# Attention products in three bursts per two rounds, row maxima in parts of 512, 512 and 1024 keys

## The chip, the core and the metric

The kernel runs on one core of one Trainium2 chip. The metric is the device time of one execution in microseconds (us). The core has TensorE (PE in the profile, with its weight loads shown apart as PEld), VectorE (DVE), ScalarE (ACT), GpSimd (POOL) and SyncE (SP, which here issues nearly all DMAs). TensorE writes its results to PSUM, which has eight banks; one bank holds 512 fp32 values on each of 128 partitions.

## The reference

Two attention blocks (A and B) of 32 heads with 16 dimensions each work on the same 2048 x 512 input, each with its own weights, and a gate per row mixes their results. Cut to what matters:

```python
def _A_ref(x, wqkv, wo):                      # _B_ref is the same with B's weights
    qkv = (x @ wqkv).reshape(B, S, 3, H, Dh)  # S = 2048, H = 32, Dh = 16
    scores = einsum("bhqd,bhkd->bhqk", q, k) * Dh ** -0.5
    p = softmax(scores, axis=-1)
    o = einsum("bhqk,bhkd->bhqd", p, v)
    return o.transpose(...).reshape(B, S, D) @ wo

g = sigmoid((x * gate_w).sum(-1, keepdims=True))
out = g * a + (1 - g) * b                     # a, b: the two blocks on A_x
```

## The kernel before

**Stages.** A prologue (up to about 294 us of the trace) makes q, k and v of both blocks (`project_qk`, `project_v`) and writes them to DRAM, q and k as a high and a low part, so that one matmul with 48 rows gives a precise product. Then 1024 rounds follow, 64 heads (both blocks) of 16 rounds each; a round r is one tile of 128 keys against all 2048 queries of a head. A tail of some 50 us finishes the output.

**One round.** It has three kinds of work:

1. *Scores and exponentials* (`scores`, L549 and L552). Four matmuls of 512 queries give the scores of 128 keys, with keys on partitions. The row maximum of each query enters as two more rows of the same matmul (50 rows in all). ACT takes each 512-wide result from its bank with one `Exp` into the tile `p`. The banks are `ps_st`, three of them in turn.
2. *Products with V* (`attend`, L521), one round behind: `acc` (one bank) collects p times V for the head. The 17 columns of V (16 and a column of ones for the sum) need few columns of the array, so four matmuls with `tile_position=(0, 32*c)` stand beside each other, one for each quarter of the queries. A *burst* is such a group: before the change it covers 256 columns of each quarter, and there are two bursts a round. The operands are plain fp32, and the trace shows each such matmul as two MATMUL records (8 records a burst).
3. *Row maxima* for a later head (`max_half`, L112 and L114), 20 rounds ahead (NT + LEAD = 16 + 4): a tile of 128 queries against all 2048 keys, as two halves of 1024 keys. A half is two matmuls of 512 into the two banks of one `ps_mx` tile (two such tiles) and one DVE `tensor_reduce` over 1024. After 16 tiles `max_split` (L124) joins the halves on DVE, POOL splits the result in two parts, and `max_rows` (L131) transposes them and sends them through DRAM into the two extra rows of `q_st`.

**Places in the array.** The stacked q and k lie twice, on partitions 0 to 49 and 64 to 113 (`HALVES`), so that two matmuls with 48 or 50 rows stand in the upper and the lower half of the array at once. Scores and maxima therefore come in pairs, and TensorE goes back and forth between this arrangement and that of the bursts.

**What sets the order.** Nothing is scheduled by a planner: each engine takes its instructions in the order in which the program issues them (`manual_schedule`), and waits come from buffers. The body of a round before is

```python
for half in range(2):
    pair(r, (2 * half, 2 * half + 1))
    if m < ROUNDS:
        max_half(m, half)
    if r:
        attend(r - 1, half)
```

A half-round is thus: a pair of scores, a pair of maxima, a burst. Work that comes now and then is in the table `later` (by round): loads of V and of output weights, denominators (`load_den`, `invert_den`), normalising, the output projection (`project_out`, 32 times within the rounds), the gate. At a head's last round ACT copies `acc` to `ev` (L538); the first burst of the next head waits for it, as there is one `acc`. While the last 20 rounds run there are no more maxima to make.

PSUM before: two `ps_mx` tiles (four banks), three `ps_st`, one `acc`. All eight are taken.

## Time and profile before

| | before |
|---|---|
| median of 3 runs | 2935.14 us (2934.06 to 2935.32) |
| the profiled execution: time, its span | 2934.63 us, 2932.8 us |
| granted TensorE clock | 0.999 |
| PE, DVE, ACT busy (share of the span) | 99%, 89%, 79% |
| DMA | 73 GB/s mean |

Busy shares are of records in the trace. Records of one engine overlap: a MATMUL's record goes from the fetch of its operands to the end of its writes, and the next one begins long before. A PE that is busy 99% of the time is therefore not a PE without gaps, and for DVE and ACT too the distance from one start to the next says more than the length of a record. The lines of the profile follow in the prediction.

### The profile page before, as it was taken

What the parts mean: (1) busy time and instruction counts of PE and PEld (TensorE: products, weight loads), DVE (VectorE), ACT (ScalarE), POOL (GpSimd) and SP (SyncE); (2) the same over time, 40 slices, a digit from 0 to 9 for tenths busy, and PEclk for the clock granted to TensorE, in tenths of its full rate; (3) what the DMA queues carried; (4) which work ended last, traced back from release to release, by engine and by line L of the source; (5) the groups of instructions that cost most, each with busy time, mean ns of one, the idle gap of its engine ahead of it and who ended that gap; (6) DMA issues with size and microseconds to landing.
All of it is one profiled execution on the core that took longest, in us unless ns stands there. A gap on an engine that the chain in (4) does not pass through costs nothing.

```text
span 2932.8 us, 61642 instructions
## 1 busy us (share of the span) xinstructions
PE 2905.4 (99%) x26192; PEld 1199.9 (41%) x26192; DVE 2618.4 (89%) x2343; ACT 2321.2 (79%) x4257; POOL 224.4 (8%) x369
## 2 busy tenths in 40 slices
PE   8999999999999999999999999999999999999999
PEld 7877333333333333333333444333333333334435
DVE  3145999999999999999999988999999999998884
ACT  3221888888888888888888776888888888887775
POOL 1000231000000000000100231000000000011201
PEclk9999999999999999999999999999999999999999
DMA  7662333222322232222323241222222233232302
GB/s 246 190 229 115 78 78 79 53 46 38 66 53 54 54 64 50 39 50 52 82 53 63 76 113 39 53 55 53 58 39 53 52 72 64 53 71 77 74 6 89
DMA packets 83753, 214.61 MB, mean 73 GB/s; under 512 B 21878, under 2 KB 32086, under 8 KB 70934
## 3 DMA queue, kind: packets, MB, share of 16 engines
q1 hardware_dynamic: 80918, 201.76, 30.1%
q0 software_dynamic: 2560, 8.91, 1.2%
q8 instruction: 206, 3.38, 0.5%
q14 instruction: 69, 0.57, 0.1%
HBM read 145.87 MB, written 64.74 MB: 72 GB/s over the span
## 4 chain that ended last, share of the span: by engine, by line
PE 95%; ACT 3%; issue 1%; DMA 1%; DVE 0%; SPq 0%
PE acc L521 38%; PE ps_st L549 29%; PE ps_mx L112 16%; PE ps_pro L195 6%; PE ps_mx L404 3%; PE ps_pro L218 3%; ACT p L552 1%; ACT ev L538 1%; DMA raw<-in_xT 0%; DMA k_st<-kd 0%; PE ps_st L404 0%; PE ps_st L455 0%; PE ps_mx L455 0%; DVE mxp L114 0%; DVE o_acc L456 0%
## 5 line engine op out<-in xcount | busy, mean ns | idle before, releaser
L114 DVE TENSOR_REDUCE mxp<-ps_mx 128x1 f32<-128x1024 f32 x2048 | 2485.9, 1222 | 41.6 <-PE ps_mx L112 40.4
L552 ACT ACTIVATE p<-ps_st 128x512 f32<-128x512 f32 x4096 | 2224.3, 596 | 360.1 <-PE ps_st L549 115.0
L521 PE MATMUL acc<-p,vg 128*17 128x256 f32 x16384 | 1285.1, 385 | 14.1 <-ACT ev L538 12.7
L549 PE MATMUL ps_st<-q_st,k_st 50*128 50x512 f32 x4096 | 1027.0, 496 | 0.0
L112 PE MATMUL ps_mx<-k_st,q_st 48*128 48x512 f32 x4096 | 821.0, 395 | 1.7 <-DVE mxp L114 1.4
L549 PEld LDWEIGHTS ps_st<-q_st,k_st 50*128 50x128 f32 x4096 | 385.3, 183 | 866.2 <-issue 453.0
L521 PEld LDWEIGHTS acc<-p,vg 128*17 128x17 f32 x16384 | 272.7, 95 | 754.8 <-issue 711.4
L112 PEld LDWEIGHTS ps_mx<-k_st,q_st 48*128 48x128 f32 x4096 | 397.6, 187 | 15.5 <-issue 9.0
L125 POOL CAST mparts<-mrow 128x16 fp32r<-128x16 f32 x64 | 12.5, 196 | 2261.8 <-DVE mrow L124 2261.8
L200 DVE TENSOR_TENSOR part<-ps_pro,part 128x1024 fp32r<-128x1024 f32 x32 | 39.2, 1224 | 109.6 <-ACT part L199 109.6
L199 ACT CAST part<-ps_pro 128x1024 fp32r<-128x1024 f32 x32 | 32.4, 1014 | 131.4 <-PE ps_pro L195 131.4
L404 PE MATMUL ps_mx<-wo,ot 128*128 128x512 f32 (+1 forms) x354 | 91.1, 402 | 0.0
L195 PE MATMUL ps_pro<-xh,whi 128*128 128x512 f32 x256 | 73.1, 405 | 7.9 <-ACT xh L181 7.5
L221 ACT COPY v_st<-ps_pro 128x512 f32<-128x512 f32 x31 | 18.2, 587 | 77.5 <-PE ps_pro L218 75.1
L404 PEld LDWEIGHTS ps_mx<-wo,ot 128*128 128x128 f32 (+1 forms) x354 | 64.0, 188 | 26.1 <-DVE mxp L114 10.2
L195 PE MATMUL ps_pro<-xh,wlo 128*128 128x512 f32 x256 | 69.4, 393 | 0.0
L195 PE MATMUL ps_pro<-xl,whi 128*128 128x512 f32 x256 | 69.3, 393 | 0.0
L195 PEld LDWEIGHTS ps_pro<-xh,whi 128*128 128x128 f32 x256 | 47.9, 191 | 22.5 <-ACT xh L181 9.9
L195 PEld LDWEIGHTS ps_pro<-xh,wlo 128*128 128x128 f32 x256 | 48.7, 190 | 10.4
L195 PEld LDWEIGHTS ps_pro<-xl,whi 128*128 128x128 f32 x256 | 48.6, 190 | 10.3
L169 DVE TENSOR_TENSOR wlo<-wraw,whi 128x512 fp32r<-128x512 f32 x16 | 10.9, 683 | 46.8 <-ACT whi L168 46.8
L408 DVE TENSOR_SCALAR o_acc<-ps_mx,gate 128x512 f32<-128x512 f32 x16 | 12.0, 751 | 35.8 <-PE ps_mx L404 35.8
(89 smaller groups left out, 603.5 us busy)
## 6 DMA issues: line engine op xcount, KB each, us to landing
k_st<-kd SPq DMA_DIRECT2D x128, 256.0 KB
q_st<-qd SPq DMA_DIRECT2D x128, 256.0 KB
qd<-part SPq DMA_DIRECT2D x32, 512.0 KB
kd<-part SPq DMA_DIRECT2D x32, 512.0 KB
k_st<-kd SPq DMA_DIRECT2D x128, 128.0 KB
q_st<-qd SPq DMA_DIRECT2D x128, 128.0 KB
od<-ev SPq DMA_DIRECT2D x63, 256.0 KB
vd<-v_st SPq DMA_DIRECT2D x32, 272.0 KB
```

What stands on the lines that cost most here:

```text
L112: pe.matmul(ps[:, c * 512:(c + 1) * 512], q[b:b + SC, t * P:(t + 1) * P], k[b:b + SC, o:o + 512], start=True, stop=True)
L114: dve.tensor_reduce(mxp[h][:, t, half:half + 1], ps, op=ALU.max, axis=AX.X)
L195: pe.matmul(ps[:, c * 512:(c + 1) * 512], a[:, k], b[:, k], start=n == 0, stop=n == 3 * KC - 1)
L199: act.copy(pt[0], ps)
L200: dve.tensor_tensor(pt[1], ps, pt[0].bitcast(F32), op=ALU.subtract)
L218: pe.matmul(ps[:, :DM], a[:, k, o:o + P], b[:, k], start=n == 0, stop=n == 3 * KC - 1)
L221: act.copy(v_st[t % 2][:, :, 0:16], v)
L404: pe.matmul(ps, ot[a][:n, slot, sl], wt[b][:n, g], start=G == groups[0] and i == 0, stop=G == groups[-1] and i == 2)
L521: pe.matmul(acc[32 * c:32 * c + 17, half * 256:(half + 1) * 256], v[:, 4 * a + c if final else kt, j], p[:, o:o + 256], start=first and ha ...
L538: act.copy(ev, acc)
L549: pe.matmul(ps[:, i * 512:(i + 1) * 512], k[b:b + SC + 2, kk * P:(kk + 1) * P], q[b:b + SC + 2, cc * 512:(cc + 1) * 512], start=True, stop ...
L552: act.activation(pt[r][:, o:o + n], ps[:, :n], AF.Exp, scale=SCALE)
```

## The change

Two rounds form one step of the loop, and a string gives the order of what PE is handed: `e` is one score matmul with its exponential, `m` a part of the maxima of 512 keys, `M` one of 1024 keys, and a digit is a burst of so many units of 128 columns. The two rounds' products come in three bursts of 384, 256 and 384 columns, and lie up to two rounds behind the scores. The maxima of one tile come as parts of 512, 512 and 1024 keys; the 512 parts use two tiles `ps_m1` of one bank, the 1024 part a single tile `ps_m2` of two banks (together the four banks that `ps_mx` had). The half of the array (`rows`) now alternates from matmul to matmul after each burst. `max_split` joins three partial maxima in place of two. In the last 20 rounds the string is `LATE`. The prologue's early maxima (`run_ahead`) are handed out in parts, `load_den` and `invert_den` move by one or two rounds, and `project_out` stands ahead of a step's first burst.

On PE, in the steady part of the rounds, these rows stood before (names: `ps_st` is a bank of scores, `ps_mx` a tile for maxima, `acc` the bank of the products, `17x256 x4` a burst):

```order
L549 MATMUL ps_st<-q_st_1967,k_st_1968 128x512 x2
L112 MATMUL ps_mx<-k_st_111,q_st_110 128x512 x2
L521 MATMUL acc<-p,vg 17x256 x4
L549 MATMUL ps_st<-q_st_1967,k_st_1968 128x512 x2
L112 MATMUL ps_mx<-k_st_111,q_st_110 128x512 x2
L521 MATMUL acc<-p,vg 17x256 x4
```

That is one round; two rounds have four bursts, each behind two pairs. Now, from a step's first burst to its third (`ps_m_` with a number is a tile of `ps_m1` or, where two matmuls write it, of `ps_m2`):

```order
L532 MATMUL acc<-p,vg 17x384 x4
L571 MATMUL ps_st<-q_st_2010,k_st_2011 128x512 x2
L123 MATMUL ps_m_18783<-k_st_114,q_st_113 128x512
L123 MATMUL ps_m_18786<-k_st_114,q_st_113 128x512
L532 MATMUL acc<-p,vg 17x128 x8
L571 MATMUL ps_st<-q_st_2010,k_st_2011 128x512
L123 MATMUL ps_m_18800<-k_st_114,q_st_113 128x512 x2
L571 MATMUL ps_st<-q_st_2010,k_st_2011 128x512
L123 MATMUL ps_m_18808<-k_st_114,q_st_113 128x512
L571 MATMUL ps_st<-q_st_2010,k_st_2011 128x512
L532 MATMUL acc<-p,vg 17x384 x4
```

Three bursts stand in two rounds, with two, three and three pairs between them. The middle burst is eight matmuls of 128 columns, since it takes the last 128 of one round and the first 128 of the next.

On DVE, in the same part, one row before was one half of 1024 keys:

```order
L114 TENSOR_REDUCE mxp_3380<-ps_mx_3517 128x1
L114 TENSOR_REDUCE mxp_3380<-ps_mx_3531 128x1
L114 TENSOR_REDUCE mxp_3380<-ps_mx_3549 128x1
L114 TENSOR_REDUCE mxp_3380<-ps_mx_3563 128x1
```

and those of two rounds are now six, four of 512 (`ps_m1`) and two of 1024 (`ps_m2`):

```order
L125 TENSOR_REDUCE mxp_10843<-ps_m2_11187 128x1
L125 TENSOR_REDUCE mxp_10843<-ps_m1_11195 128x1
L125 TENSOR_REDUCE mxp_10843<-ps_m1_11208 128x1
L125 TENSOR_REDUCE mxp_10843<-ps_m2_11214 128x1
L125 TENSOR_REDUCE mxp_10843<-ps_m1_11232 128x1
L125 TENSOR_REDUCE mxp_10843<-ps_m1_11235 128x1
```

The same columns are read, in six instructions where there were four, and the two large ones have one tile between them.

The diff:

```diff
--- before.py
+++ after.py
@@ -58,7 +58,8 @@
     const = ctx.enter_context(tc.tile_pool(name="const", bufs=1))
     small = ctx.enter_context(tc.tile_pool(name="small", bufs=2))
     dram = ctx.enter_context(tc.tile_pool(name="dram", bufs=1, space=DRAM))
-    ps_mx = ctx.enter_context(tc.tile_pool(name="ps_mx", bufs=2, space=PSUM))
+    ps_m1 = ctx.enter_context(tc.tile_pool(name="ps_m1", bufs=2, space=PSUM))
+    ps_m2 = ctx.enter_context(tc.tile_pool(name="ps_m2", bufs=1, space=PSUM))
     qd = [[dram.tile([2, HG, DH, S], F32, name=f"qd{s}{g}") for g in range(NG)] for s in range(2)]
     kd = [[dram.tile([2, HG, DH, S], F32, name=f"kd{s}{g}") for g in range(NG)] for s in range(2)]
@@ -99,19 +100,29 @@
             dma(k[b + 32:b + 48].bitcast(F32), ks[0, j])
             dma(q[b + 32:b + 48].bitcast(F32), qs[1, j])
+    PARTS = ((0,), (1,), (2, 3))
     mxp = {}
-    def max_half(m, half):
+    turn = [0]
+    def rows():
+        turn[0] ^= 1
+        return HALVES[1 - turn[0]]
+    def max_part(m, part):
         h, t = divmod(m, NT)
-        if t == 0 and half == 0:
-            mxp[h] = small.tile([P, NT, 2], F32, name="mxp")
+        if t == 0 and part == 0:
+            mxp[h] = small.tile([P, NT, 3], F32, name="mxp")
         q, k = q_st[h % 3], k_st[h % 3]
-        ps = ps_mx.tile([P, 1024], F32, name="ps_mx")
-        for c in range(2):
-            o, b = half * 1024 + c * 512, HALVES[c]
-            pe.matmul(ps[:, c * 512:(c + 1) * 512], q[b:b + SC, t * P:(t + 1) * P], k[b:b + SC, o:o + 512],
-                      start=True, stop=True)
-        dve.tensor_reduce(mxp[h][:, t, half:half + 1], ps, op=ALU.max, axis=AX.X)
+        chunks = PARTS[part]
+        n = len(chunks)
+        ps = (ps_m1 if n == 1 else ps_m2).tile([P, n * 512], F32, name=f"ps_m{n}")
+        for i, c in enumerate(chunks):
+            b = rows()
+            pe.matmul(ps[:, i * 512:(i + 1) * 512], q[b:b + SC, t * P:(t + 1) * P],
+                      k[b:b + SC, c * 512:(c + 1) * 512], start=True, stop=True)
+        dve.tensor_reduce(mxp[h][:, t, part:part + 1], ps, op=ALU.max, axis=AX.X)
@@ -121,7 +132,7 @@
         halves = mxp.pop(h)
         m = small.tile([P, NT], F32, name="mrow")
         mp = small.tile([P, 2, NT], F32R, name="mparts")
-        dve.tensor_tensor(m, halves[:, :, 0], halves[:, :, 1], op=ALU.max)
+        dve.tensor_reduce(m, halves, op=ALU.max, axis=AX.X)
         pool.tensor_copy(mp[:, 0], m)
         pool.tensor_tensor(mp[:, 1], m, mp[:, 0].bitcast(F32), op=ALU.subtract)
         mparts[h] = mp
@@ -211,7 +222,7 @@
             hi, lo = wblocks[s, 2 * DM]
             c, o = divmod(t * P, 512)
             last = s == 1 and t == NT - 1
-            ps = ps_mx.tile([P, 1024], F32, name="ps_mx") if last else ps_pro.tile([P, 1024], F32, name="ps_pro")
+            ps = ps_m1.tile([P, 512], F32, name="ps_m1") if last else ps_pro.tile([P, 1024], F32, name="ps_pro")
             n = 0
             for a, b in ((xh[c], hi), (xl[c], hi), (xh[c], lo)):
                 for k in range(KC):
@@ -236,13 +247,14 @@
             split_x(c, 2, load_x(c, 2))
             if c < 3:
                 block(load_w, c)
-        ahead = [(m, half) for m in range(NT + LEAD) for half in range(2)]
+        ahead = [(m, part) for m in range(NT + LEAD) for part in range(3)]
         def run_ahead(n):
-            for _ in range(min(n, len(ahead))):
-                m, half = ahead.pop(0)
-                max_half(m, half)
-                if (m, half) == (NT - 1, 1):
+            turn[0] = 0
+            for _ in range(n):
+                m, part = ahead.pop(0)
+                max_part(m, part)
+                if (m, part) == (NT - 1, 2):
                     max_split(0)
                     pending.append(0)
@@ -254,7 +266,7 @@
                 load_w(i // 8, 2 * DM, DM)
             if i in (4, 9):
                 split_w(i // 8, 2 * DM, DM)
-            project_qk(s, g, isk, lambda: run_ahead(i >= 10))
+            project_qk(s, g, isk, lambda: run_ahead((i >= 10) + (i >= 13)))
             if i in (5, 6, 8, 9):
                 load_stacks(i // 8, HALVES[(i - 5) % 3:][:1])
             if i == 7:
@@ -270,7 +282,7 @@
                 if pending[0] == 3:
                     max_rows(pending.pop() - 3)
             if t and t != NT - 2:
-                run_ahead(2)
+                run_ahead(3)
         assert not ahead and not pending
@@ -389,7 +401,7 @@
     def result_bank():
         banks.append(len(banks) % 5)
         if banks[-1] % 2 or not fill_only:
-            return ps_mx.tile([P, 1024], F32, name="ps_mx")[:, :DM]
+            return ps_m1.tile([P, 512], F32, name="ps_m1")
         return ps_st.tile([P, 512], F32, name="ps_st")
     def project_out(side, t):
@@ -475,7 +487,7 @@
         end = (G + 1) * HG * NT
         at(end + 2, load_den, G)
         at(end + 10, invert_den, G, 0)
-        at(end + 11, invert_den, G, 1)
+        at(end + 12, invert_den, G, 1)
     for side in range(2):
         groups = SIDES[side]
         end = (groups[-1] + 1) * HG * NT
@@ -489,9 +501,9 @@
             for i in range(4):
                 at(end + 42 + 16 * c + 2 * i, project_out, side, 4 * c + i)
     end = ROUNDS - NT
-    at(end + 1, load_den, LAST)
+    at(end + 2, load_den, LAST)
     for i in range(2):
-        at(end + 3, invert_den, LAST, i)
+        at(end + 4, invert_den, LAST, i)
     fill = []
     for c in range(NQ):
         at(end + 4 + c // 2, load_num, LAST, c)
@@ -509,7 +521,7 @@
-    def attend(r, half):
+    def attend(r, qa, qb):
         h, kt = divmod(r, NT)
         v, j = vg[h // HG], h % HG
         p = pt[r]
@@ -517,11 +529,10 @@
         a = kt % 4
         first, last = (a == 0, a == 3) if final else (kt == 0, kt == NT - 1)
         for c in range(NQ):
-            o = c * 512 + half * 256
-            pe.matmul(acc[32 * c:32 * c + 17, half * 256:(half + 1) * 256],
-                      v[:, 4 * a + c if final else kt, j], p[:, o:o + 256],
-                      start=first and half == 0, stop=last, tile_position=(0, 32 * c), skip_group_check=True)
-        if half == 0:
+            pe.matmul(acc[32 * c:32 * c + 17, qa * P:qb * P], v[:, 4 * a + c if final else kt, j],
+                      p[:, c * 512 + qa * P:c * 512 + qb * P], start=first and qa == 0, stop=last,
+                      tile_position=(0, 32 * c), skip_group_check=True)
+        if qb < 4:
             return
         del pt[r]
         if final and last:
@@ -538,49 +549,69 @@
             act.copy(ev, acc)
             nc.sync.dma_start(od[G][j].rearrange("c r t -> (c r) t"), ev)
+    done = [0]
+    def attend_next(n):
+        while n:
+            r, qa = divmod(done[0], 4)
+            qb = min(4, qa + n)
+            attend(r, qa, qb)
+            done[0] += qb - qa
+            n -= qb - qa
+    def score(r, c):
+        h, kt = divmod(r, NT)
+        if c == 0:
+            pt[r] = ppool.tile([P, S], F32, name="p")
+        q, k = q_st[h % 3], k_st[h % 3]
+        kk, cc = (4 * (kt % 4) + c, kt // 4) if h == NH - 1 else (kt, c)
+        b = rows()
+        ps = ps_st.tile([P, 512], F32, name="ps_st")
+        pe.matmul(ps, k[b:b + SC + 2, kk * P:(kk + 1) * P], q[b:b + SC + 2, cc * 512:(cc + 1) * 512],
+                  start=True, stop=True)
+        act.activation(pt[r][:, c * 512:(c + 1) * 512], ps, AF.Exp, scale=SCALE)
+    FULL = "e3eemm2eMeme3emeM"
+    LATE = "ee2ee2ee2ee2"
     after = {}
-    def scores(r, chunks, ps):
+    for r in range(0, ROUNDS, 2):
         h, kt = divmod(r, NT)
-        q, k = q_st[h % 3], k_st[h % 3]
-        for i, c in enumerate(chunks):
-            kk, cc = (4 * (kt % 4) + c, kt // 4) if h == NH - 1 else (kt, c)
-            b = HALVES[c % 2]
-            pe.matmul(ps[:, i * 512:(i + 1) * 512], k[b:b + SC + 2, kk * P:(kk + 1) * P],
-                      q[b:b + SC + 2, cc * 512:(cc + 1) * 512], start=True, stop=True)
-        o, n = chunks[0] * 512, len(chunks) * 512
-        act.activation(pt[r][:, o:o + n], ps[:, :n], AF.Exp, scale=SCALE)
-    def one():
-        return ps_st.tile([P, 512], F32, name="ps_st")
-    def pair(r, chunks):
-        for c in chunks:
-            scores(r, (c,), one())
-    for r in range(ROUNDS + 1):
-        for fn, a in later.pop(r, ()):
-            fn(*a)
-        h, kt = divmod(r, NT)
+        projects = []
+        for rr in (r, r + 1):
+            for fn, a in later.pop(rr, ()):
+                if fn is project_out:
+                    projects.append(a)
+                else:
+                    fn(*a)
+        if kt == 0 and h + 2 < NH:
+            load_stacks(h + 2)
         m = r + NT + LEAD
-        if r < ROUNDS:
-            if kt == 0 and h + 2 < NH:
-                load_stacks(h + 2)
-            pt[r] = ppool.tile([P, S], F32, name="p")
-            for half in range(2):
-                pair(r, (2 * half, 2 * half + 1))
-                if m < ROUNDS:
-                    max_half(m, half)
+        scored = parts = 0
+        for step in FULL if m < ROUNDS else LATE:
+            if step == "e":
+                score(r + scored // 4, scored % 4)
+                scored += 1
+            elif step in "mM":
+                max_part(m + parts // 3, parts % 3)
+                parts += 1
+            else:
+                for a in projects:
+                    project_out(*a)
+                projects = []
+                turn[0] = 0
                 if r:
-                    attend(r - 1, half)
-            if m < ROUNDS and m % NT == NT - 1:
-                max_split(m // NT)
-                after[r + 1] = m // NT
-        else:
-            attend(r - 1, 0)
-            attend(r - 1, 1)
-        if r in after:
-            max_rows(after.pop(r))
+                    attend_next(int(step))
+                if scored > 1 and r in after:
+                    max_rows(after.pop(r))
+        m += 1
+        if m < ROUNDS and m % NT == NT - 1:
+            max_split(m // NT)
+            after[r + 2] = m // NT
+    attend_next(8)
     fill_only.append(True)
     for fn, *a in fill:
         fn(*a)
```

## The prediction

> **What bounds the kernel now.** I read the page's busy shares first, then its chain that ended last, then its groups by line.
>
> ```profile
> PE 2905.4 (99%) x26192; PEld 1199.9 (41%) x26192; DVE 2618.4 (89%) x2343; ACT 2321.2 (79%) x4257; POOL 224.4 (8%) x369
> PE 95%; ACT 3%; issue 1%; DMA 1%; DVE 0%; SPq 0%
> PE acc L521 38%; PE ps_st L549 29%; PE ps_mx L112 16%; PE ps_pro L195 6%; PE ps_mx L404 3%; PE ps_pro L218 3%; ACT p L552 1%; ACT ev L538 1%; DMA raw<-in_xT 0%; DMA k_st<-kd 0%; PE ps_st L404 0%; PE ps_st L455 0%; PE ps_mx L455 0%; DVE mxp L114 0%; DVE o_acc L456 0%
> L114 DVE TENSOR_REDUCE mxp<-ps_mx 128x1 f32<-128x1024 f32 x2048 | 2485.9, 1222 | 41.6 <-PE ps_mx L112 40.4
> L552 ACT ACTIVATE p<-ps_st 128x512 f32<-128x512 f32 x4096 | 2224.3, 596 | 360.1 <-PE ps_st L549 115.0
> L521 PE MATMUL acc<-p,vg 128*17 128x256 f32 x16384 | 1285.1, 385 | 14.1 <-ACT ev L538 12.7
> ```
>
> The chain is PE for 95%, and 83% of it lies in the three lines of the rounds. DVE looks nearly as full: 2048 reductions of 1.22 us. But it is on the chain for 0%, so its 1.22 has to be looked at again below. The rounds decide, and a timeline of PE alone shows one half-round after the other (columns: start, length, line, count):
>
> ```profile
> 1499.92 0.50 PE L549 MATMUL ps_st<-q_st,k_st 50*128 50x512 f32 x2
> 1500.26 0.40 PE L112 MATMUL ps_mx<-k_st,q_st 48*128 48x512 f32 x2
> 1500.58 0.63 PE L521 MATMUL acc<-p,vg 128*17 128x256 f32 x8
> 1501.14 0.50 PE L549 MATMUL ps_st<-q_st,k_st 50*128 50x512 f32 x2
> 1501.48 0.40 PE L112 MATMUL ps_mx<-k_st,q_st 48*128 48x512 f32 x2
> 1501.81 0.62 PE L521 MATMUL acc<-p,vg 128*17 128x256 f32 x8
> ```
>
> From start to start: pair of scores to pair of maxima 0.34 us, maxima to burst 0.33, burst to next scores 0.56; 1.22 in all, 4.88 for two rounds. How much of that is columns? The prologue has matmuls of 512 columns in one unbroken row:
>
> ```profile
> 249.37 1.07 PE L218 MATMUL ps_pro<-wvhi,xl 128*128 128x512 f32 x4
> 250.28 1.07 PE L218 MATMUL ps_pro<-wvlo,xh 128*128 128x512 f32 x4
> ```
>
> Four take 0.91, so 0.23 each, weight loads hidden. A pair (side by side) is then 0.23, and a burst's two passes are 0.23 each: its eight records end 0.63 after the start, the last 0.385 long, so the second pass begins 0.24 after the first. Columns account for 4 x 0.23 = 0.91 of the 1.22. The other 0.31 is paid where the arrangement of the array changes: 0.11 ahead of the first pair (its weight load stands open), 0.10 between maxima and burst, 0.10 behind the burst. **A burst costs 0.31 beside its columns.**
>
> **The change, part by part.**
>
> *One burst fewer in two rounds.* PE saves 0.31. The columns stay: 8 score and 8 maximum matmuls (8 pairs) and 1024 columns per quarter in two passes. The 384 bursts take 0.10 + 3/2 x 0.46 = 0.79 where a 256 burst takes 0.56. The middle burst is two lots of 128, so four passes where two stood. The trace has no pass of 128 columns. The nearest are matmuls of two columns, each with a weight load of 128 columns:
>
> ```profile
> 2906.00 0.25 PE L442 MATMUL ps_mx<-pick,ev_hi 128*128 128x2 f32 x1
> 2906.11 0.25 PE L442 MATMUL ps_mx<-pick,ev_lo 128*128 128x2 f32 x1
> ```
>
> They follow at 0.11, so two more passes cost between 0 and 0.22. Here only 17 columns of weights are loaded, 17/128 of that load, so I take 0.03. PE alone: 4.88 - 0.31 + 0.03 = **4.60**. Pairs now mix a score with a maximum; both kinds already run side by side in halves of the array, so I take nothing, below or above, for that.
>
> *DVE: six reductions where four stood.* After an interruption DVE has a backlog, and then its own pace shows:
>
> ```profile
> 644.48 0.17 DVE L124 TENSOR_TENSOR mrow<-mxp 128x16 f32<-128x16 f32 x1
> 644.57 2.35 DVE L114 TENSOR_REDUCE mxp<-ps_mx 128x1 f32<-128x1024 f32 x2
> 646.83 0.20 DVE L131 STREAM_TRANSPOSE mt<-mparts 128x32 f32<-128x32 f32 x1
> 646.96 5.70 DVE L114 TENSOR_REDUCE mxp<-ps_mx 128x1 f32<-128x1024 f32 x5
> ```
>
> Two reductions take 644.57 to 646.83, that is 1.13 from start to start; the records overlap by 0.09, and in an ordinary half-round of 1.22 DVE has that much to spare. For 512 columns the groups by form give the slope:
>
> ```profile
> L169 DVE TENSOR_TENSOR wvlo<-raw,wvhi 128x2048 fp32r<-128x2048 f32 x2 | 4.6, 2292 | 1.0 <-ACT wvhi L168 1.0
> L182 DVE TENSOR_TENSOR xl<-raw,xh 128x1024 fp32r<-128x1024 f32 x6 | 7.3, 1225 | 5.3 <-ACT xh L181 5.0
> L182 DVE TENSOR_TENSOR xl<-raw,xh 128x512 fp32r<-128x512 f32 x4 | 2.7, 692 | 1.5 <-ACT xh L181 1.5
> L317 DVE TENSOR_REDUCE logit<-xsum 128x16 f32<-128x512 f32 x1 | 0.7, 675 | 0.0
> ```
>
> 2292 - 1225 = 1067 ns for 1024 columns, so 512 fewer take 533 off: 1.13 - 0.53 = **0.60**. The one reduction of 512 in the trace lasts 0.675; less the overlap of 0.09 it is 0.59. Below it cannot go under the 0.53 of its columns; above stands this row, of another operation that reads 512 columns from PSUM:
>
> ```profile
> 1682.53 0.75 DVE L408 TENSOR_SCALAR o_acc<-ps_mx,gate 128x512 f32<-128x512 f32 x1 [2.27 <-PE ps_mx L404]
> 1683.20 1.22 DVE L114 TENSOR_REDUCE mxp<-ps_mx 128x1 f32<-128x1024 f32 x1
> ```
>
> There the next start is 0.67 later. Two rounds on DVE: 2 x 1.13 + 4 x 0.60 = 4.66 (4.38 to 4.94). The join and the transposition of a head (0.09 and 0.13 from start to start by the rows of that backlog) add 0.03 per step: **4.69**, under 4.88 and over PE's 4.60. DVE, nowhere on the chain before, comes within a few hundredths of being the bound.
>
> The Trainium skill, "Perfetto Trace Analysis", section "Optimizing Scalar/DVE Operations", gives a DVE instruction on PSUM about 125 ns of engine time beside its columns. By that figure, as an estimate, a step would need 2 x 1.19 + 4 x 0.66 = 5.02 and the change would lose. The backlog above shows 1.13 - 1.07 = 0.06 for a reduction out of PSUM, half of it, so the trace does not agree.
>
> *One tile for the large parts.* PE may refill `ps_m2` only when its reduction is over. The latencies:
>
> ```profile
> 294.18 2.35 DVE L114 TENSOR_REDUCE mxp<-ps_mx 128x1 f32<-128x1024 f32 x2 [3.97 <-PE ps_mx L112]
> 295.46 0.19 PEld L112 LDWEIGHTS ps_mx<-k_st,q_st 48*128 48x128 f32 x2 [0.74 <-DVE mxp L114]
> 1012.38 0.40 PE L112 MATMUL ps_mx<-k_st,q_st 48*128 48x512 f32 x2
> 1012.83 1.22 DVE L114 TENSOR_REDUCE mxp<-ps_mx 128x1 f32<-128x1024 f32 x1 [0.26 <-PE ps_mx L112]
> ```
>
> A reduction starts 0.45 after its matmul and lasts 1.22; PE's next load into the tile starts 0.06 after its end (294.18 + 1.22 = 295.40, then 295.46). So from the second matmul of the `M` in the step's second stretch, PE must wait 0.45 + 1.22 + 0.06 = 1.73 before it loads for the `M` in the third. What PE has in between: a pair (0.23), the way into the burst (0.33), the 384 burst (0.79), then the `e m` pair (0.34 until the next pair streams, whose load would begin 0.11 sooner): 0.23 + 0.33 + 0.79 + 0.34 - 0.11 = 1.58. The load comes 0.15 late, and PE takes instructions in order, so the next step's scores stand behind it: **+0.15**. From the third stretch back to the second of the next step lie over 2.5 us; there is no wait. PE's period becomes 4.60 + 0.15 = **4.75**, with DVE (4.69) and ACT under it:
>
> ```profile
> 295.24 1.09 ACT L552 ACTIVATE p<-ps_st 128x512 f32<-128x512 f32 x2 [0.87 <-PE ps_st L549]
> ```
>
> Two exponentials in 1.09, each 0.60 long, start 0.49 apart; eight are 3.92. But three banks `ps_st` make one place tight: the last `e` of the second stretch needs the exponential of the third `e` before it, which ends 0.45 + 0.49 + 0.60 + 0.06 = 1.60 after the first pair behind burst one, and its load is due after 0.23 + 0.33 + 0.59 + 0.11 + 0.23 + 0.23 - 0.11 = 1.61. No wait, and no room.
>
> *Ends of heads.* The first burst of a head waits for the copy of `acc`:
>
> ```profile
> PE acc L521 <- ACT ev L538: 12.7, 63, 0.5
> ```
>
> Two pairs stood between the bursts there, now three and the wait of 0.15, so most of 12.7 us goes: -10 (0 to -13). ACT has the room for the copy.
>
> *The rest.* In the prologue a call of `run_ahead` may hold one part, which costs a whole pair: 4 more pairs of 0.23, +1 us. At the end two rounds of products stand without cover instead of one, four passes of 0.23, +1 us, and the first step has none. The projections (L404) keep their matmuls and go from beside a burst to beside a burst. Denominators move by a round behind a head and are due long after. The maxima's way through DRAM (SP's DMAs behind the transposition) starts about 1.5 steps, 7 us, ahead of the head's first score, as three rounds of 2.44 were before. I take nothing for these.
>
> *Sum.* Steps with maxima: (1024 - 20) / 2 = 502. 502 x (4.75 - 4.88) = -65; ends of heads -10; prologue and end, as the products that the first step lacks come back there, +1. 2934.6 (the profiled execution: its span 2932.8 and 1.8 around it) - 74 = **2860**; that execution lies 0.5 under the median of the runs, which is nothing here.
>
> **The rivals.**
>
> 1. *The wait for `ps_m2` hides.* If the latencies in it come out 0.1 shorter, DVE's 4.69 is the period: -95, -10, so 2830; with parts at 0.59 it is 4.65 and 2810. For it: the wait is small. Against: it follows from latencies that every step repeats.
> 2. *A second wait in the step.* The `e` without room comes 0.10 late (a copy of `acc`, a late `M`), or the narrow passes take 0.1 more: 4.85, -15, -10, so 2910. For it: three loops (PE 4.75, DVE 4.69, the `ps_st` banks) lie within 0.1 of each other, and a delay in one is no longer absorbed. At 4.88 nothing is won.
> 3. *Slower: DVE's fixed cost per reduction isn't overlapped.* The small parts wait on semaphores twice as often; where their records of 0.69 (the 512 row above) stand end to end, DVE needs 2 x 1.13 + 4 x 0.69 = 5.02, +0.14 x 502 = +70, -10 at the heads, so 2995. It decides from (4.88 - 2.26) / 4 = 0.655 for a part. For it: the 0.67 behind L408. Against: every backlog in the trace overlaps, and L317. The figure of the Trainium skill above would give this time too.
> 4. *The middle burst doesn't count as one.* At 0.22 for its passes: 4.60 + 0.19 + 0.15 = 4.94, +30 - 10, so 2955. Against: second passes with new weights already follow at 0.24.
>
> **How the numbers follow.** Forecast 60% (2835 to 2885, for steps of 4.70 to 4.80). Rival 1 12% (2810 to 2835), rival 2 14% (2885 to 2935), rival 3 11%, rival 4 3%. A measurement of this kernel can tell about 0.2% (6 us) from no change; from rival 2, 9% is still faster and 5% is not: faster 81%, same 5%, slower 14%. The range, 2815 to 2930, takes in nearly all of rival 1 and of rival 2, and leaves out the slower ones and the ends of the others, 2 in 10.
>
> **What would show it.** Burst records three to two rounds, scores 0.31 after a burst's last start as before, and pairs at 0.23 inside a stretch: the saving is right. DVE starts 0.60 behind a 512 part with a backlog: the price is right; 0.66 or more and rival 3 holds. PE's wait on DVE for `ps_m2`, some 0.15 in each of 502 steps, is the loop; none of it is rival 1, waits on ACT for `ps_st` at many steps are rival 2. A step away from 4.70 to 4.80 makes the forecast wrong.

## The result, and the profile after

| | before | after |
|---|---|---|
| median | 2935.23 us (4 runs, 2934.06 to 2939.06) | 2853.9 us (4 runs, 2852.81 to 2855.59) |
| ratio, 95% interval | | 0.9721 [0.9704, 0.9738] |
| profiled execution: time, span | 2934.63 us, 2932.8 us | 2855.59 us, 2853.8 us |
| granted TensorE clock | 0.999 | 0.998 |

The change takes 81 us off; 74 were forecast. The page of the changed kernel has these lines (busy shares, chain by engine and by line, two of the groups):

```profile
PE 2835.5 (99%) x26176; PEld 1378.6 (48%) x26176; DVE 2556.1 (90%) x3367; ACT 2264.3 (79%) x4257; POOL 225.0 (8%) x369
PE 92%; DVE 6%; DMA 1%; ACT 0%; issue 0%; SPq 0%; ACTq 0%; DVEq 0%
PE acc L532 35%; PE ps_st L571 30%; PE ps_m L123 14%; DVE mxp L125 6%; PE ps_pro L206 6%; PE ps_m L416 3%; PE ps_pro L229 3%; DMA raw<-in_xT 1%; PE ps_st L416 0%; DVE rn L371 0%; PE ps_st L467 0%; ACT p L573 0%; PE ps_m L467 0%; DVE o_acc L468 0%; PE ps_m L229 0%
L532 PE MATMUL acc<-p,vg 128*17 128x384 f32 (+1 forms) x16368 | 1186.7, 384 | 1.9 <-ACT ev L540 1.4
```

The shares hardly differ from before. What is new is `DVE mxp L125 6%` in the chain: the chain now passes through the maxima's reductions, which stood at 0% before. The wait of PE on ACT's copy at the ends of heads has gone from 12.7 us to 0.5 in all (the 1.4 in the row is at L540, the copies of the last head, and stood there before too). The groups by form, and the waits, of the same kernel:

```profile
L125 DVE TENSOR_REDUCE mxp<-ps_m 128x1 f32<-128x512 f32 x2048 | 1312.3, 682 | 44.6 <-PE ps_m L123 44.5
L125 DVE TENSOR_REDUCE mxp<-ps_m 128x1 f32<-128x1024 f32 x1024 | 1245.2, 1216 | 6.3 <-PE ps_st L571 0.9
PEld ps_st L571 <- ACT p L573: 731.6, 1487, 1.3
PEld ps_m L123 <- DVE mxp L125: 37.8, 125, 0.8
```

DVE stands idle ahead of its reductions for 51 us in all, in the whole program. The two wait rows need care: the row on ACT looks like the bound and, as the experiments show, is not, and the row on DVE, which is the wait that was forecast for every step, counts only 125 of them. The timeline shows why. This is PE over one ordinary step of two rounds (start, length, line, count; `...` marks rows left out). What stands between two bursts is called a stretch below:

```profile
1503.22 0.84 PE L532 MATMUL acc<-p,vg 128*17 128x384 f32 x8
1503.99 0.50 PE L571 MATMUL ps_st<-q_st,k_st 50*128 50x512 f32 x2
...
1504.64 0.63 PE L532 MATMUL acc<-p,vg 128*17 128x128 f32 x16
1505.20 0.49 PE L571 MATMUL ps_st<-q_st,k_st 50*128 50x512 f32 x1
1505.21 0.72 PE L123 MATMUL ps_m<-k_st,q_st 48*128 48x512 f32 x2
...
1506.09 0.84 PE L532 MATMUL acc<-p,vg 128*17 128x384 f32 x8
1506.86 0.50 PE L571 MATMUL ps_st<-q_st,k_st 50*128 50x512 f32 x1
...
1507.24 0.58 PE L123 MATMUL ps_m<-k_st,q_st 48*128 48x512 f32 x2
1507.58 0.40 PE L571 MATMUL ps_st<-q_st,k_st 50*128 50x512 f32 x1
1507.91 0.52 PE L532 MATMUL acc<-p,vg 128*17 128x384 f32 x4
```

Read from start to start: burst 0.77, two pairs and the way into the burst 0.65, middle burst 0.56, three pairs 0.89, burst 0.77, three pairs 1.05: together 4.69, where it was 4.88. The second and the third stretch have the same work; the third is 0.16 longer. Its `M` stands late, at 1507.24. The rows of weight loads and of DVE at that place say what it waited for:

```profile
1506.97 0.19 PEld L571 LDWEIGHTS ps_st<-q_st,k_st 50*128 50x128 f32 x1
1507.24 0.19 PEld L123 LDWEIGHTS ps_m<-k_st,q_st 48*128 48x128 f32 x2
1505.96 3.55 DVE L125 TENSOR_REDUCE mxp<-ps_m 128x1 f32<-128x1024 f32 x4
```

The reduction of the step's first `M` starts at 1505.96 and is 1.22 long, so it ends at 1507.18, and the load of the next `M` follows 0.06 later. That is the loop of the single `ps_m2`. Between the two loads only 0.08 us are without a record (1507.16 to 1507.24), so the list of waits hardly shows it: a wait of 0.1 inside a dense stretch is read from distances.

For all the runs below, "the step" is the distance from the middle burst of a step to that of the next (with four bursts, from a burst to the fourth behind it), as the median over those steps that hold nothing else. Before, it is 4.88, after 4.70. From the first score of round 0 to that of round 1004, all 502 steps take 2560.6 us before and 2479.6 after, 5.10 and 4.94 in the mean: 81 us less. The ordinary part is 0.18 x 502 = 90 us, so some 9 us are given back in special steps. Per head (eight steps) the special steps cost, above the ordinary ones:

| us per head | before | after |
|---|---|---|
| first use of a new head's stacks | 0.14 | 0.05 |
| join and transposition of the maxima | 0 | 0.25 |
| around the copy of `acc` | 0.27 | 0.15 |

So the ends of heads, where 10 us were to be won, cost 0.41 a head before and 0.45 after. Another 5 us are given back where a group of heads ends: `invert_den` puts two reciprocals on DVE, seven times in the program.

```profile
632.49 0.54 DVE L371 RECIPROCAL rn<-dn 128x64 f32<-128x64 f32 x1
637.77 0.54 DVE L371 RECIPROCAL rn<-dn 128x64 f32<-128x64 f32 x1
```

The steps that hold them are 0.35 and 0.40 longer than others in their place; in the kernel before they are no longer at all. The remaining few us lie in single steps and were not followed up. Errors stood against each other in the forecast: ordinary steps gave 25 us more than the 65 expected, and the special ones took 9 where 10 were to be won. That 2860 came so near to 2854 is in part luck.

### The profile page after: what moved, and what is told of

Read it like the earlier page. It is cut to its first block, busy times and chain, and to the rows that moved or that the text cites. A ratio compares the mean times of both kernels' runs of the same rounds, so it can differ in the third digit from the quotient of the medians.

```text
span 2853.8 us, 62585 instructions
## 1 busy us (share of the span) xinstructions
PE 2835.5 (99%) x26176; PEld 1378.6 (48%) x26176; DVE 2556.1 (90%) x3367; ACT 2264.3 (79%) x4257; POOL 225.0 (8%) x369
## 4 chain that ended last, share of the span: by engine, by line
PE 92%; DVE 6%; DMA 1%; ACT 0%; issue 0%; SPq 0%; ACTq 0%; DVEq 0%
PE acc L532 35%; PE ps_st L571 30%; PE ps_m L123 14%; DVE mxp L125 6%; PE ps_pro L206 6%; PE ps_m L416 3%; PE ps_pro L229 3%; DMA raw<-in_xT 1%; PE ps_st L416 0%; DVE rn L371 0%; PE ps_st L467 0%; ACT p L573 0%; PE ps_m L467 0%; DVE o_acc L468 0%; PE ps_m L229 0%
## 5 line engine op out<-in xcount | busy, mean ns | idle before, releaser
L125 DVE TENSOR_REDUCE mxp<-ps_m 128x1 f32<-128x512 f32 (+1 forms) x3072 | 2419.3, 860 | 50.9 <-PE ps_m L123 44.5
L573 ACT ACTIVATE p<-ps_st 128x512 f32<-128x512 f32 x4096 | 2168.0, 599 | 335.9 <-PE ps_st L571 234.8
L571 PE MATMUL ps_st<-q_st,k_st 50*128 50x512 f32 x4096 | 1332.3, 446 | 0.1
L123 PE MATMUL ps_m<-k_st,q_st 48*128 48x512 f32 x4096 | 1200.0, 435 | 3.1 <-DVE mxp L125 2.7
L532 PE MATMUL acc<-p,vg 128*17 128x384 f32 (+1 forms) x16368 | 1186.7, 384 | 1.9 <-ACT ev L540 1.4
L571 PEld LDWEIGHTS ps_st<-q_st,k_st 50*128 50x128 f32 x4096 | 597.1, 184 | 763.4 <-ACT p L573 731.6
L123 PEld LDWEIGHTS ps_m<-k_st,q_st 48*128 48x128 f32 x4096 | 543.7, 185 | 105.2 <-DVE mxp L125 37.8
L532 PEld LDWEIGHTS acc<-p,vg 128*17 128x17 f32 x16368 | 314.9, 96 | 509.8 <-issue 483.7
L210 ACT CAST part<-ps_pro 128x1024 fp32r<-128x1024 f32 x32 | 32.5, 1015 | 132.0 <-PE ps_pro L206 132.0
L416 PE MATMUL ps_m<-wo,ot 128*128 128x512 f32 (+1 forms) x354 | 90.6, 401 | 0.0
L416 PEld LDWEIGHTS ps_m<-wo,ot 128*128 128x128 f32 (+1 forms) x354 | 63.9, 188 | 23.9 <-DVE mxp L125 8.7
```

Source lines behind the costliest of these rows:

```text
L123: pe.matmul(ps[:, i * 512:(i + 1) * 512], q[b:b + SC, t * P:(t + 1) * P], k[b:b + SC, c * 512:(c + 1) * 512], start=True, stop=True)
L125: dve.tensor_reduce(mxp[h][:, t, part:part + 1], ps, op=ALU.max, axis=AX.X)
L210: act.copy(pt[0], ps)
L416: pe.matmul(ps, ot[a][:n, slot, sl], wt[b][:n, g], start=G == groups[0] and i == 0, stop=G == groups[-1] and i == 2)
L532: pe.matmul(acc[32 * c:32 * c + 17, qa * P:qb * P], v[:, 4 * a + c if final else kt, j], p[:, c * 512 + qa * P:c * 512 + qb * P], start=fi ...
L571: pe.matmul(ps, k[b:b + SC + 2, kk * P:(kk + 1) * P], q[b:b + SC + 2, cc * 512:(cc + 1) * 512], start=True, stop=True)
```

## The experiments

The theory as of the prediction: PE bounded the kernel before, one burst fewer saves its switch, and what bounds it now is the loop of `ps_m2`. The main rival: DVE, which has hardly a gap, bounds it now.

**Which engine, which parts.** Three kernels let DVE read fewer columns, so that it gets faster while PE's work stays. `light_m` halves the small parts, `light_M` the large one, `light_mM` both:

```diff
 # light_m
-        dve.tensor_reduce(mxp[h][:, t, part:part + 1], ps, op=ALU.max, axis=AX.X)
+        src = ps[:, :256] if n == 1 else ps
+        dve.tensor_reduce(mxp[h][:, t, part:part + 1], src, op=ALU.max, axis=AX.X)
 # light_M:   src = ps if n == 1 else ps[:, :512]
 # light_mM:  src = ps[:, :256] if n == 1 else ps[:, :512]
```

> The reductions of the 512 parts read 256 of their 512 columns, so half of these keys don't enter the row maxima; PE's instructions and their order are those of the change. DVE's work per step falls from 4.69 us to about 2 x 1.13 + 4 x 0.33 = 3.6 us, while the reduction of the 1024 part keeps its length. Loop theory (the single ps_m2 tile sets the step: matmul, 1.22 us of reduction, next load): the step stays at 4.68 to 4.70 us, the time at 2840 to 2856. DVE theory (six reductions fill DVE, PE only follows): the step falls to PE's own 4.53 to 4.60 us, the time to 2770 to 2805.

> The reductions of the 1024 part read 512 of their 1024 columns, so half of these keys don't enter the row maxima. This shortens the loop over ps_m2 by 0.53 us and DVE's step to 2 x 0.60 + 4 x 0.60 = 3.6 us. Loop theory and DVE theory both say that the step falls to PE's own 4.53 us, the time to about 2770. A third theory (the three ps_st banks hold the step) says that less is won: 4.59 us and 2800 where scores wait for exponentials, or nothing where they already set 4.70.

> Both kinds of reduction read half of their columns, so half of the keys don't enter the row maxima. DVE's step is 2 x 0.60 + 4 x 0.33 = 2.5 us and the loop over ps_m2 has 0.4 us to spare. What is left is PE with its switches (4.53 us, time 2770) or the exponentials' three banks (4.59 us, 2800). If light_M already gives this time, the small parts' price doesn't matter once the loop is open.

Measured: 2835.16, 2786.83 and 2786.34 us (before, on the same chip: 2934.64). With half of the small parts gone DVE had over 1 us of room in a step, and the step stayed at 4.70; the 19 us came from the heads (the step with the join went from 4.95 to 4.70, and those with the reciprocals were no longer than others in their place). With the large part halved, the step was 4.58, and halving the small ones as well changed nothing. So in ordinary steps DVE's work as a whole isn't the bound of the changed kernel; the one reduction that holds the single tile is. PE's timeline of `light_M` shows what it costs:

```profile
1499.52 0.84 PE L533 MATMUL acc<-p,vg 128*17 128x384 f32 x8
...
1501.51 0.50 PE L572 MATMUL ps_st<-q_st,k_st 50*128 50x512 f32 x1
...
1502.41 0.84 PE L533 MATMUL acc<-p,vg 128*17 128x384 f32 x8
1503.18 0.50 PE L572 MATMUL ps_st<-q_st,k_st 50*128 50x512 f32 x1
...
1504.10 0.84 PE L533 MATMUL acc<-p,vg 128*17 128x384 f32 x8
```

The third stretch is 0.92 here (1503.18 to 1504.10) and 1.05 in the changed kernel; the second, 0.90, didn't move. So PE without any wait needs 4.58, and the wait is 0.12 a step, 60 us. All of that is not to be had by opening the loop alone: `light_M` also takes 1 us of work a step off DVE, whose own floor in the changed kernel is found below at 4.65. The expectation also named a lower step of 4.53; it was not reached. In this run the weight loads' wait on ACT is still there, nearly as large:

```profile
PEld ps_st L572 <- ACT p L574: 718.6, 1424, 1.3
```

So that row, 0.5 us a time behind a burst, is only the name of what came last while PE was busy with the burst; a release isn't a wait unless something stands ready for it.

**Was PE the bound before?** `before_light` is the kernel before with half of each reduction:

```diff
-        dve.tensor_reduce(mxp[h][:, t, half:half + 1], ps, op=ALU.max, axis=AX.X)
+        dve.tensor_reduce(mxp[h][:, t, half:half + 1], ps[:, :512], op=ALU.max, axis=AX.X)
```

> The kernel before, with its reductions reading 512 of the 1024 columns, so half of the keys don't enter the row maxima. The prediction says that PE with four bursts in two rounds sets 4.88 us there and DVE has 0.09 us to spare in a half-round: the step stays at 4.88, the time between 2915 and 2936 (a little off where DVE's join disturbs a head). If DVE had held the kernel before, it would fall below 2900.

Measured: 2929.92 us, the step 4.88 as before. DVE, 89% busy, was not the bound; of the 5 us nearly 3 lie in the very first step. Beside `light_M` this run also gives the price of a burst: DVE is out of the way in both, and the step is 4.88 with four bursts and 4.58 with three.

**Each half of the change alone.** `bursts_alone` has the three bursts and keeps the halves of 1024 keys in two tiles; `parts_alone` has the new parts and tiles, and four bursts:

```diff
 # bursts_alone (with two ps_mx tiles of 1024 in place of ps_m1 and ps_m2)
-    PARTS = ((0,), (1,), (2, 3))
+    PARTS = ((0, 1), (2, 3))
-    FULL = "e3eemm2eMeme3emeM"
+    FULL = "3MeeM2eeMe3eeMe"
 # parts_alone
-    FULL = "e3eemm2eMeme3emeM"
+    FULL = "eemm2eeM2eemm2eeM2"
```

> Three bursts in two rounds as in the change, but the maxima as halves of 1024 keys in two tiles, as before (DVE 4 x 1.13 = 4.53 us a step, less than the change's 4.66). Between three bursts four halves cannot be spread evenly: two of them fall into one stretch. If switches alone count, PE's 4.58 us of light_M holds: about 2785. If the maxima's tiles and DVE's pace must fit the stretches, the gain is lost: a timetable from the latencies gives 4.89 us, 2925 to 2950.

> Maxima in parts of 512, 512 and 1024 keys with the new tiles, but four bursts of 256 columns in two rounds, in the order of before. PE's four switches stay, 4.88 us a step; DVE needs 4.66 + 0.03, less than that, and the large parts lie 2.44 us apart, more than the 1.73 of their loop. Expected: no change, 2925 to 2942. If the parts themselves brought something, it would be faster than 2920; if DVE's smaller parts disturb, slower than 2945.

Measured: `bursts_alone` 2935.27 us, ratio 0.9999 [0.999, 1.0008], the step 4.915. `parts_alone` 2963.8 us, ratio 1.01 [1.0083, 1.0117], the step 4.88. In these orders neither half gains anything by itself. The 29 us that `parts_alone` loses are a side effect of its order: `project_out` stands there right behind two `m` and wants a tile `ps_m1`. The 32 steps with a projection grew from 7.50 to 8.39 in the mean, and the waits show the new line:

```profile
PEld ps_m L416 <- DVE mxp L125: 28.3, 24, 1.2
PE ps_m L416 <- DVE mxp L125: 25.8, 32, 0.9
```

"No change" was right for its ordinary steps and wrong for its total. Whether `bursts_alone` failed for its halves or for its order was then open, so `bursts_halves` has the same tiles and another order, with each `M` placed by the latencies of the prediction:

```diff
 # against bursts_alone
-    FULL = "3MeeM2eeMe3eeMe"
+    FULL = "3eMe2eMee3MeeMe"
```

> Three bursts with the maxima as halves of 1024 keys again, but in another order than bursts_alone, 3eMe2eMee3MeeMe: stretches of four, five and seven matmuls, in which the halves lie further apart. It asks whether bursts_alone showed a property of halves or of its order. If halves cannot be fitted whatever the order, 4.88 us or more, 2925 to 2940. A timetable from the latencies gives 4.76 us for this order, 0.12 less than before: 2870 to 2885, still behind the change.

Measured: 2912.6 us (2906.67 to 2918.15), ratio 0.9918 [0.9897, 0.9939], the step 4.788, against 4.76 by the latencies. So order was most of it, and halves of 1024 can have half of the gain in the step. The total fell short of its expectation: the step with the join is 5.07, and others with special work are longer too.

**How near is DVE?** `extra_dve` adds one small transposition to every step, on tiles that nothing else uses:

```diff
+        dve.transpose(idle[1], idle[0])
         m += 1
```

> The change with one more DVE instruction a step, a transposition of 128 x 32 (0.125 us from start to start), at the step's end. The loop over ps_m2 sets 4.70 us and DVE's own work is 4.66 to 4.69: with next to no room, the step grows by about 0.09 to 0.12 us, the time by 45 to 60 to 2897 to 2915. If DVE had 0.1 us or more to spare, the time stays at 2852 to 2860.

Measured: 2868.38 us, +14.5, the step 4.745. The size was missed by a factor of three or more. (0.045 x 502 would be 23 us; the steps at the ends of heads and those with a projection grew less or not at all.) DVE's rows say why (columns: start, length, line, count):

```profile
1499.82 1.81 DVE L125 TENSOR_REDUCE mxp<-ps_m 128x1 f32<-128x512 f32 x2
1501.55 0.20 DVE L612 STREAM_TRANSPOSE idle<-idle 128x32 f32<-128x32 f32 x1
1501.67 4.70 DVE L125 TENSOR_REDUCE mxp<-ps_m 128x1 f32<-128x512 f32 x6
```

DVE is full now. Its starts lie 0.598, 0.597, 1.132, 0.125 (the transposition), 0.564, 0.598 and 1.131 apart, 4.745 together, and that is the step. The added instruction is 0.20 in its record, takes 0.125, and the reduction behind it has the next start 0.033 sooner, so its net price is 0.092. DVE's own floor without it is 4.745 - 0.092 = 4.653: in the changed kernel it had 0.045 to spare, where the expectation had put it at 4.66 to 4.69.

**Where the 10 us at the ends of heads went.** `short_copy` shortens ACT's copy of `acc` (the other columns are filled with ones), and `no_join` takes the join of the partial maxima off DVE (two of the three parts are left out):

```diff
 # short_copy
-            act.copy(ev, acc)
+            pool.memset(ev[:, 64:], 1.0)
+            act.copy(ev[:, :64], acc[:, :64])
 # no_join
-        dve.tensor_reduce(m, halves, op=ALU.max, axis=AX.X)
+        pool.tensor_copy(m, halves[:, :, 2])
```

> At a head's end ACT copies 64 of the 512 columns of acc (the others are filled with ones, so that the output is not that of the reference); the copy holds ACT for about 0.09 us where it held it for 0.465. The theory is that the wait for acc that the prediction took away (12.7 us) came back as scores that wait for their banks behind the copy on ACT, 0.15 us in the step after a head's end: then this step falls to 4.70 and the time by about 9 us, to 2845. If the copy was hidden anyway, nothing changes (2852 to 2858).

> The change without the join of a head's partial maxima on DVE (GpSimd copies the part of the last 1024 keys alone, so the other keys don't enter the row maxima). The step in which join and transposition fall takes 4.95 us where others take 4.70. Theory: DVE, without room, passes the join's 0.12 us on to PE: the step falls by 0.10 to 0.15 us, 63 heads by 6 to 10 us, to 2844 to 2848. Rival: the 0.25 comes from the new head's stacks or the transposition, and the time stays at 2852 to 2856.

Measured: 2843.3 and 2843.41 us, 10.6 and 10.5 under the changed kernel. In `short_copy` the step behind a head's end went from 4.85 to 4.70, an ordinary one. In `no_join` the step of the join went from 4.95 to 4.73. What the copy does in the changed kernel is seen on ACT and on PE:

```profile
1298.06 0.60 ACT L549 COPY ev<-acc 128x512 f32<-128x512 f32 x1
1298.53 2.66 ACT L573 ACTIVATE p<-ps_st 128x512 f32<-128x512 f32 x5
1299.57 0.64 PE L571 MATMUL ps_st<-q_st,k_st 50*128 50x512 f32 x2
...
1300.37 0.63 PE L532 MATMUL acc<-p,vg 128*17 128x128 f32 x16
```

The exponential behind the copy starts 0.47 later than it would, its bank `ps_st` comes free later, and the short stretch of two pairs takes 0.80 (1299.57 to 1300.37) where it takes 0.65 otherwise. PE waits no longer for the copy, but for the exponential behind the copy. And the join:

```profile
1284.79 1.21 DVE L125 TENSOR_REDUCE mxp<-ps_m 128x1 f32<-128x1024 f32 x1
1286.04 0.20 DVE L135 TENSOR_REDUCE mrow<-mxp 128x16 f32<-128x48 f32 x1
1286.16 1.28 DVE L125 TENSOR_REDUCE mxp<-ps_m 128x1 f32<-128x512 f32 x2
1287.36 0.20 DVE L142 STREAM_TRANSPOSE mt<-mparts 128x32 f32<-128x32 f32 x1
1287.48 4.73 DVE L125 TENSOR_REDUCE mxp<-ps_m 128x1 f32<-128x1024 f32 x6
```

The join starts 1.25 behind the reduction of an `M`, where 1.13 is usual: it begins only behind the end of that record (1284.79 + 1.21 = 1286.00). With its own 0.12 it costs DVE 0.24, and the transposition 0.09 net, as above. This pushes the reduction of the next `M` back, which is the one inside the loop, and PE's `M` behind it: 0.25 in that step. With DVE at 4 x 1.13 = 4.53 in a step of 4.88 there was room for both in the kernel before; with 4.65 in 4.70 there is none.

**Another order.** Two kernels change the order in the string alone, `order_mMm` also which keys form the large part:

```diff
 # order_422
-    FULL = "e3eemm2eMeme3emeM"
+    FULL = "4meMee2meem2eMeem"
 # order_mMm: that string too, and
-    PARTS = ((0,), (1,), (2, 3))
+    PARTS = ((0,), (1, 2), (3,))
```

> The change with another string alone: 4meMee2meem2eMeem, bursts of 512, 256 and 256 columns, none split between two rounds, the large parts in the first and the third stretch. Loop theory: two bursts or a burst of 512 now lie between one large part and the next, more than the 1.73 us that the loop over ps_m2 takes, so its wait is gone and DVE's own 4.65 us sets the step (0.05 less than 4.70): 20 to 25 us less than the change, 2828 to 2836. If the scores' three banks wait in this order, or the projections are late, it is no better or slower, 2852 to 2880. If DVE had room, as a plain count of switches says, 4.58 and 2790.

Measured: 2969.74 us, ratio 1.0114 [1.0099, 1.013], the step 5.00: a miss, and my own. The letters `m` and `M` only count; the sizes come from `PARTS` in turn (512, 512, 1024). The order that ran was `m e m e e`, `M e e m`, `e m e e M`, with 5, 5 and 6 matmuls between the bursts. A stretch of 5 takes 0.89 and 0.90, as long as one of 6 without a wait: the unpaired matmul costs a whole slot. The last takes 1.10. With `PARTS` made to fit, the string gives bursts of 512, 256 and 256 columns with stretches of 6, 4 and 6:

> The order that order_422 was meant to have. There the string named the large part second, but sizes come from the table PARTS, which has it third, so the large parts stood elsewhere and two stretches had five matmuls. Here PARTS is 512, 1024, 512 and the string 4meMee2meem2eMeem: stretches of six, four and six, bursts of 512, 256 and 256. Between one large part and the next lie two bursts or a burst of 512. Loop theory: the wait for ps_m2 is gone, DVE's 4.65 to 4.68 us sets the step: 2830 to 2848, 0.2 to 0.8% under the change. If the loop was not what set 4.70, the time stays at 2850 to 2860; if this order starves the scores' banks, above 2870.

Measured: 2821.42 us (2821.07 to 2823.19), ratio **0.9611 [0.9598, 0.9624]**, better than both kernels and than its own expectation. Its chain and a row of its waits:

```profile
DVE 77%; PE 20%; issue 1%; DMA 0%; ACT 0%; SPq 0%; DVEq 0%
PEld ps_m L123 <- DVE mxp L125: 557.5, 913, 1.7
```

The large part now comes in the first and in the third stretch. PE's timeline has its pairs of matmuls at

```profile
1505.15 0.45 PE L123 MATMUL ps_m<-k_st,q_st 48*128 48x512 f32 x2
...
1507.55 0.73 PE L123 MATMUL ps_m<-k_st,q_st 48*128 48x512 f32 x2
...
1509.83 0.43 PE L123 MATMUL ps_m<-k_st,q_st 48*128 48x512 f32 x2
```

so its uses are 2.40 and 2.28 apart, where the changed kernel has 2.03 (1505.21 to 1507.24, the wait within it) and the rest of the step. The loop is open, and DVE is the bound at last: 77% of the chain. Its step is 4.655, which is the floor of 4.653 that `extra_dve` gave. Against the changed kernel the ordinary steps give 0.045 x 502 = 23 us and the heads, 0.32 above ordinary in place of 0.45, 8 us: 31 of the 32.5.

## Why the prediction was right

- **The switch of a burst.** Right. 0.31 was read from the distances before, and PE alone was put at 4.60 for a step; `light_M` shows 4.58, 0.30 under `before_light`.
- **The narrow passes.** 0.03 was taken, 0 to 0.22 was open. The middle burst takes 0.56 from start to start, as one of 256 columns did: nothing. Rival 4 falls.
- **DVE's price.** Right: 0.60 and 1.13 were forecast, 0.598 and 1.132 measured, and 4.66 for the step against 4.653. Rival 3 falls. The 125 ns beside the columns that the Trainium skill gives ("Perfetto Trace Analysis", "Optimizing Scalar/DVE Operations") don't show: 1.132 - 0.598 = 0.534 for 512 columns leaves 0.06 of 0.598.
- **The loop of `ps_m2`.** Right in place and mechanism: +0.15 forecast, 0.16 between the two like stretches, 0.12 against the kernel without it.
- **The size of the step.** 4.75 was forecast and 4.70 measured. The terms that were mis-sized are PE's own 4.60 (it is 4.58) and the wait (0.12, not 0.15). 0.05 x 502 is the 25 us, and 4.70 is the very edge of the 4.70 to 4.80 that the prediction allowed itself.
- **The ends of heads, -10.** This step failed. It was argued that most of the 12.7 us wait goes and that ACT has the room for the copy. The wait went, from 12.7 to 0.5 us, but the copy's 0.47 came back through the banks `ps_st`, of which the prediction itself says that they have no room. And the join and the transposition, which were spread as 0.03 over all steps, fall in one step where DVE has 0.045 free. They were also read too low: 0.09 and 0.13 leave out that the join starts only behind the end of the reduction ahead of it (before the change too: the two reductions ahead of the join at 644.48 run from 642.16 to 644.44); measured are 0.24 and 0.09. The copy and the join are worth some 10.5 us each, as `short_copy` and `no_join` show, one run each. A cost that comes once in eight steps can't be averaged against a slack that exists per step.
- **Denominators, for which nothing was taken.** The reciprocals cost 5 us, again for want of room on DVE: in `light_m` they cost nothing.
- **Rivals 1 and 2.** Rival 1's step (DVE's 4.69) lies nearer to the measured 4.70 than the forecast's 4.75, but `light_m` shows that DVE isn't the cause; the state that rival 1 describes is what `order_mMm` reaches. Rival 2's sign was to be waits on ACT for `ps_st` at many steps. The list has them, 731.6 us, and they cost nothing in ordinary steps. As a sign it was badly chosen.

Outside of the steps the span lost 2 us in place of the 1 that was forecast (79 us less in the span, 81 in the steps): the first score of the rounds starts 2.1 us later.

## What to carry to other kernels

Where a tile has one buffer, add up what its engine has to do between two uses, and compare it with fill, read and release; that sum told the place of the wait here to 0.03 us, and moving the tile in the order removed it. When two engines come within 1% of each other, price each rare instruction against the slack of the step that it falls in, not against the mean. And before you trust a string or a table that sets an order, write out what it really issues.

## What the runs showed of the hardware

- Four-pass bursts of 128 columns with their own weight loads take as long (0.56) as two passes of 256.
- Pairs count, not matmuls: 5 matmuls in the two halves of the array take the time of 6 (0.89).
- A small DVE instruction between long ones has a record of 0.20, a distance of 0.125 and a net price of 0.092, since the start behind its successor comes 0.033 sooner.
